# Pooled attention and an MLP mixer: u kept as pairs of token chunks, and its transpose by way of memory

## The chip, the cores and the metric

The kernel runs on one core of one Trainium2 chip. The metric is the device time of one execution in microseconds, the median of several runs. The engines are called PE (TensorE matmuls; PEld its weight loads), DVE (VectorE), ACT (ScalarE), POOL (GpSimd) and SP (SyncE, which here only issues DMAs).

## What is computed

Eight batches (B = 8), eight heads, 576 tokens, 64 features a head. Keys and values are pooled by 8 along the sequence, attention runs over the 72 pooled keys, and its output x (576 tokens x 512 features per batch) goes through a mixer: a token MLP, then a channel MLP, each with a residual.

```python
def _attn_ref(q, k, v):
    k_p = k.reshape(B, H, Sp, pool, D).mean(axis=3)
    v_p = v.reshape(B, H, Sp, pool, D).mean(axis=3)
    scores = scale * np.matmul(q, k_p.transpose(0, 1, 3, 2))
    ...
    return np.matmul(attn, v_p)

def _moe_ref(x, w_tok1, w_tok2, w_ch1, w_ch2):
    xt = x.transpose(0, 2, 1)
    h = np.maximum(xt @ w_tok1, 0.0) @ w_tok2
    u = x + h.transpose(0, 2, 1)
    h2 = np.maximum(u @ w_ch1, 0.0) @ w_ch2
    return u + h2
```

w_tok1 is 576 x 256, w_tok2 256 x 576, w_ch1 512 x 1536, w_ch2 1536 x 512. Inputs and output are float32; inside, operands are bf16 and sums float32.

## The kernel before

**Tiling.** The 576 tokens of a batch are 64 x 9: token p * 9 + r. A chunk c (0 to 3) holds the 128 tokens with r = 2c and 2c + 1; the 64 tokens with r = 8 are the batch's tail. Tails of two batches fill one 128-row tile ("xt", then a row of `u_tails`), so that after eight batches the tails make four chunks of a ninth unit of work.

**Stages of a batch.** Scores and exp (`s0` to `s3`), attention output (`av0` to `av4`, PE at L317, DVE at L329 and L335), token MLP (`at0`, `at1`: L363, L354), and u (`u0` to `u4`: two matmuls at L378 and an add on DVE at L379 for each chunk). For the tails, `u4` is done once for two batches, with four matmuls whose weights `w_tok2t` are zero in the other batch's 64 columns.

**uT.** The channel MLP needs u with features on the partitions. Batch 0 gets it another way; batches 1 to 3 by PE transposes (`t0` to `t4`, L388, weights = u, and a DVE copy, L389). Batches 4 to 7 go through memory: `M0`, `M2` and (odd batches) `M4` spill u and the pair of tails to the DRAM tile `mem` (L397); `M` reads it back in four DMAs (L404), each for a quarter of the features, in runs of 128 elements, to `v`; `T0` to `T4` are DVE 32x32 block transposes from `v` to `uT` (L411, on 32-bit pairs of features) and `uT_tails` (L417, on bf16). Because a 32-bit element holds two neighbouring features of one token, `uT` of these batches has two features side by side, and `moving` (L464 to L468) reads every second element.

**Units.** `unit(n)` is the channel MLP of batch n, for n = 8 that of the tails. First product: `l1_tile` (from L470), 48 matmuls of 128 x 512 at L473 into 12 tiles, each evicted with a relu by ACT to `GT` (L477). Second product: unit 0 does it plainly (L496); units 1 to 8 (`unit_fast`, from L536) use seven block products instead of eight, in a Strassen-like scheme: `product` issues 84 matmuls of 128 x 256 at L545, whose weights are 128-column slices of `GT` or of sums of its parts (`fast["S"]`, in the tile "area", made by DVE at L516 and L523 in `g_sums`), and `plus` (L566) adds u and partial results on DVE. `store` (L487) writes two DMAs per pair of chunks from SP; in unit 8 the last two chunks are stored by `store_part` (L578), each half of the columns and each chunk by itself.

**Order.** It is written out by hand: each engine executes in the order in which the program issues. A unit is a generator that yields some 48 times (after every two matmuls of the first product, every four of the second); at the yield with number i, the steps that a table lists for i are issued: steps of the next batch (no mark), of this one ("<"), of the one after next (">"), loads ("lk3": load k of batch n + 3), `g_sums` ("=1a") and `gate` ("g0"), which lets POOL go on. `FIRST`, `SECOND`, `THIRD` and `LAST` are the tables of units 0, 1, 2 and 8, `LATER` that of units 3 to 7. So unit n works on batch n and prepares u and uT of batch n + 1 and the attention of batch n + 2. `u4`, `t4`, `M4` and `T4` are left out for even batches. SP's queue holds the spills, the reads and the stores in program order; POOL's holds the loads of inputs and the pooling.

Of the kernel before, what the change touches and what calls it, by code (L numbers as in the profile page):

```python
# [22 lines left out]
FIRST = {0: "<u0", 2: "<u3", 6: "k1", 10: "lv2", 15: "K0 Q0", 16: "kpT Q1 lk3", 18: "V0 s1 <u2", 20: "s0",  # L23
         22: "lq3 v1 s2", 24: ">K0 s3", 25: "av1", 26: "av4", 27: "<u1 av3 av2", 30: ">K1", 32: "av0", 36: "at0 at1",
         38: "u3 >V0", 40: "u4 u0", 44: "lv3 u2 u1", 45: "t3 t0", 46: "t1", 47: "t2 t4"}
SECOND = {4: "g0", 7: ">K0 kpT", 8: "Q1", 9: "Q0", 11: "s2", 12: ">Q0", 13: ">Q1", 14: "v1 =3a s0", 15: "lv3 lk3",
          16: "s1", 17: "=1a", 18: "s3 =3b", 19: "av1", 20: "av3", 21: "av2", 22: "lq3", 23: ">K1 av0", 24: "av4",
          26: "g1", 27: "=1b", 28: ">kpT =2a", 29: "at0", 30: ">s3", 31: "=2b", 32: "=4b at1 =4a", 34: ">s2",
          36: "u2", 38: ">V0", 39: "u0 >s1 u3", 40: "t2", 41: "u1 t3", 42: ">s0 >V1 t0 t1"}
THIRD = {0: ">K0 av4 lk3 lq3", 2: "av3", 4: ">K1", 6: "av0", 9: "av2", 10: ">V0 av1", 12: "=3b", 14: "at0 at1",  # L30
         15: "=3a", 16: ">kpT", 17: "g0", 18: ">Q0", 19: "=1a u3 >s1", 20: ">Q1", 23: "u1 >s3 =2a", 24: "u0 =1b u2",
         25: "=2b t1", 26: ">s0", 28: "u4 >s2 =4b", 29: ">V1", 30: "=4a g1", 33: "t0", 34: "t2 >av3", 35: "t3",
         37: ">av4", 39: "t4 >av1", 41: "lv3", 42: ">av2", 44: ">av0"}
LATER = {0: ">Q0", 6: "=3a >K0", 7: "at0 at1", 8: ">K1 >kpT", 9: ">V0 u1 u0 >Q1", 10: "u3 >s1", 11: ">V1 u4",
         12: "u2", 13: ">s0", 14: "M0", 15: "M4 M2", 16: "M", 17: ">s3 lk3", 18: "=3b", 20: "=1a", 21: "g0",
         22: ">av3 =2a", 23: "=1b", 24: "lq3", 25: "=2b", 27: ">s2 =4a", 28: "=4b", 31: "g1 >av2", 36: ">av4",
         38: "T1 T3", 39: "T2", 40: "T0", 43: ">av0", 44: ">av1 lv3 T4"}
LAST = {14: "=3b", 22: "=1a", 24: "=2a =1b", 25: "=4a", 28: "=2b", 31: "=4b", 34: "=3a"}
PLANS = {0: FIRST, 1: SECOND, 2: THIRD, 8: LAST}


@with_exitstack
def kernel(
# [44 lines left out]
    w_tok2t = singles.tile([P, 2, 2, P], BF16)  # L88
# [8 lines left out]
    u_tails = singles.tile([P, 4, DM], BF16)  # L97
# [50 lines left out]
    def permute_tok2():  # L148
        src = f2.rearrange("t m (p r) -> t m r p", r=BR)
        dst = w_tok2.rearrange("t m (r p) -> t m r p", p=BP)  # L150
        for m in range(2):
            nc.gpsimd.tensor_copy(out=dst[:, m], in_=src[:, m])
        for half in range(2):
            nc.gpsimd.tensor_copy(out=w_tok2t[:, :, half, half * BP:(half + 1) * BP], in_=w_tok2[:, :, 8 * BP:S])
# [25 lines left out]
    def batch_steps(b):  # L180
# [19 lines left out]
        def late(key):  # L200
            if key not in st:
                pool, shape = {"x": (mix, [P, 4, DM]), "u": (mix, [P, 4, DM]), "uT": (mix, [P, 4, 4 * P]),
                               "AT": (att, [P, 2, DM]), "qD": (att, [P, 2, S, 2])}[key]
                st[key] = pool.tile(shape, BF16, name=key)
            return st[key]

        def parts(src):
            return src.rearrange("p (m k) -> p k m", k=4)

# [158 lines left out]
        def u(c):  # L368
            def go():
                ps = ps_one.tile([P, 512], FP32, name="p1")  # L370
                if c < 4:
                    mms = [(w_tok2[:, m, c * P:(c + 1) * P], st["AT"][:, m, :]) for m in range(2)]
                    dst, x = late("u")[:, c, :], st["x"][:, c, :]
                else:
                    mms = [(w_tok2t[:, m, half, :], tails[b // 2, half][:, m, :]) for half in range(2) for m in range(2)]
                    dst, x = u_tails[:, b // 2, :], st["xt"]
                for i, (w, a) in enumerate(mms):
                    nc.tensor.matmul(out=ps, lhsT=w, rhs=a, start=(i == 0), stop=(i == len(mms) - 1))  # L378
                nc.vector.tensor_tensor(out=dst, in0=ps, in1=x, op=ALU.add)  # L379
            return go  # L380

        def uT(c):
            def go():
                src = st["u"][:, c, :] if c < 4 else u_tails[:, b // 2, :]
                dst, o = (late("uT"), c * P) if c < 4 else (uT_tails, b // 2 * P)
                ps = ps_one.tile([P, 4, P], BF16, name="p1")
                for kk in range(4):
                    nc.tensor.transpose(out=ps[:, kk, :], in_=parts(src)[:, kk], identity=ident)  # L388
                nc.vector.tensor_copy(out=dst[:, :, o:o + P], in_=ps)  # L389
            return go  # L390

        def spill(i):
            def go():
                if "mem" not in st:
                    st["mem"] = hbm.tile([5, P, DM], BF16, name="mem")
                src = st["u"][:, 2 * i:2 * i + 2, :] if i < 2 else u_tails[:, b // 2:b // 2 + 1, :]
                nc.sync.dma_start(out=st["mem"][2 * i:min(2 * i + 2, 5)].rearrange("c p n -> p c n"), in_=src)  # L397
            return go

        def quads():  # L400
            n = 4 + par
            st["v"] = swap.tile([P, 4 * 5, P], BF16, name="v")
            for a in range(4):
                nc.sync.dma_start(out=st["v"][32 * a:32 * a + 32, 0:4 * n, :],  # L404
                                  in_=st["mem"][0:n, :, a * P:(a + 1) * P].rearrange("c (i t) f -> t (c i) f", i=4))

        def blocks(c):
            def go():
                if c < 4:
                    st["paired"] = True  # L410
                    nc.vector.transpose(  # L411
                        out=late("uT").rearrange("f k n -> f (k n)").bitcast(U32).rearrange(
                            "f (k c a t) -> f k c a t", k=2, c=4, a=4)[:, :, c].rearrange("f k a t -> f a k t"),
                        in_=st["v"][:, 4 * c:4 * c + 4, :].bitcast(U32).rearrange("t a (f k) -> t a k f", k=2))
                    return
                dst, o = uT_tails, b // 2 * P
                nc.vector.transpose(out=dst[:, :, o:o + P].rearrange("f k (a t) -> f a k t", a=4),  # L417
                                    in_=st["v"][:, 4 * c:4 * c + 4, :].rearrange("t a (f k) -> t a k f", k=4))
# [32 lines left out]
        for c in range(5):  # L451
            name[f"av{c}"], name[f"u{c}"], name[f"t{c}"] = av(c), u(c), uT(c)
            name[f"aw{c}"] = av(c, True)
            name[f"at_{c}"], name[f"T{c}"] = at_tile(c), blocks(c)
# [4 lines left out]
        name["M"] = quads  # L459
# [4 lines left out]
    def moving(u):  # L464
        if "paired" not in u:
            return [u["uT"][:, kk, :] for kk in range(4)]
        pairs = u["uT"].rearrange("f k n -> f (k n)").rearrange("f (k n e) -> f k n e", k=2, e=2)
        return [pairs[:, kk // 2, :, kk % 2] for kk in range(4)]  # L468
# [20 lines left out]
    def unit_plain(n, u):  # L489
        uT = moving(u)  # L490
        for m in range(NM):
            yield from l1_tile(n, m, uT)
        for c in range(4):
# [8 lines left out]
            nc.vector.tensor_tensor(out=o[:, c % 2], in0=ps, in1=u["u"][:, c, :], op=ALU.add)  # L502
# [33 lines left out]
    def unit_fast(n, u):  # L536
        last = n == B
        uT = moving(u)
# [3 lines left out]
        def product(ps, a, w, start, after, split=False):  # L542
            for i in range(2):
                for m in range(NH):
                    nc.tensor.matmul(out=ps[i] if split else ps[:, i], lhsT=a(m)[:, i * P:(i + 1) * P], rhs=w(m),  # L545
# [26 lines left out]
        def store_part(cols):  # L572
            def go(i):
                if not last:
                    return
                c = 2 + i
                for half in range(2):
                    (nc.scalar if half else nc.sync).dma_start(  # L578
                        out=out[2 * c + half].rearrange("(p r) n -> p r n", r=BR)[:, 8, cols],
                        in_=ob[half * BP:(half + 1) * BP, i, cols])  # L580
# [3 lines left out]
        u1, u2 = u["u"][:, 0:2], u["u"][:, 2:4]  # L584
# [18 lines left out]
        if last:  # L603
            yield from product(x, lambda m: SG[:, 2, m], lambda m: TW[:, 2, m], False,
                               plus(ob[:, :, hi], x, s5, store_part(hi)), True)
            yield from product(x, lambda m: GT[:, NH + m, hi], lambda m: TW[:, 3, m], False,
                               plus(ob[:, :, lo], x, u2[:, :, lo], store_part(lo)), True)
# [25 lines left out]
    def unit(n, at):  # L633
        if n + 2 < B:
            batches[n + 2][0]()
        st = batches[n][2] if n < B else dict(uT=uT_tails, u=u_tails)
# [5 lines left out]
        for i, _ in enumerate((unit_fast if n >= 1 else unit_plain)(n, st)):  # L642
            for s in at.get(i, "").split():
                if s[0] == "=":
                    g_sums(s[1:])
                    continue
                if s[0] == "l":
                    load(s[1], n + int(s[2]))
                    continue
                if s[0] == "g":  # L650
                    gate()
                    continue
                ahead = {"<": 0, ">": 2}.get(s[0], 1)
                s = s.lstrip("<>")
                if n + ahead < B and ((n + ahead) % 2 or s not in ("u4", "t4", "M4", "T4")):
                    batches[n + ahead][1][s]()

    with tc.manual_schedule(engines={PE, POOLE, DVE, ACT, SYNC}):
# [10 lines left out]
        nc.vector.memset(w_tok2t, 0.0)  # L669
# [13 lines left out]
        for n in range(B + 1):  # L683
            unit(n, PLANS.get(n, LATER))
# [30 lines left out]
```

## Time and profile before

| | |
|---|---|
| median of 3 runs | 278.35 us (278.29 to 280.8) |
| span of the profiled execution | 276.3 us |
| granted clock of TensorE | 0.995 of full speed |
| PE / DVE / ACT / POOL busy | 261.1 / 193.0 / 113.6 / 144.8 us |
| DMA | 36,455 packets, 32.71 MB, 13,776 of them under 512 bytes |

The costliest groups of the steps concerned (line, engine, operation, destination and sources, shapes, count; then busy us and mean ns of one; then idle time of the engine before them and what ended it):

```profile
L473 PE MATMUL p<-uT,w_ch 128*128 128x512 bf16 x366 | 91.8, 383 | 2.7 <-DVE uT L411 1.1
...
L545 PEld LDWEIGHTS <-area 128*128 128x128 bf16 x384 | 36.6, 98 | 5.1 <-issue 0.5
L545 PE MATMUL p<-area,area 128*128 128x256 bf16 x288 | 36.2, 273 | 0.0
...
L379 DVE TENSOR_TENSOR u<-p,x 128x512 bf16<-128x512 f32 x32 | 21.5, 684 | 13.5 <-PE p L378 13.3
...
mem<-u SPq DMA_DIRECT2D x8, 256.0 KB, 2.1
v<-mem SPq DMA_DIRECT2D x8, 160.0 KB, 6.7
v<-mem SPq DMA_DIRECT2D x8, 128.0 KB, 5.3
```

A matmul's duration in such a row includes its way through the array; matmuls overlap, and what one costs TensorE is the distance from one start to the next. In the last three rows the numbers are the KB of one DMA and the median time from issue to landing.

### The profile page before, as it was taken

What the parts mean: (1) busy time and instruction counts of PE and PEld (TensorE: products, weight loads), DVE (VectorE), ACT (ScalarE), POOL (GpSimd) and SP (SyncE); (2) the same over time, 40 slices, a digit from 0 to 9 for tenths busy, and PEclk for the clock granted to TensorE, in tenths of its full rate; (3) what the DMA queues carried; (4) which work ended last, traced back from release to release, by engine and by line L of the source; (5) the groups of instructions that cost most, each with busy time, mean ns of one, the idle gap of its engine ahead of it and who ended that gap; (6) DMA issues with size and microseconds to landing.
All of it is one profiled execution on the core that took longest, in us unless ns stands there. A gap on an engine that the chain in (4) does not pass through costs nothing.

```text
span 276.3 us, 5208 instructions
## 1 busy us (share of the span) xinstructions
PE 261.1 (95%) x2064; PEld 156.1 (57%) x2092; DVE 193.0 (70%) x378; ACT 113.6 (41%) x200; POOL 144.8 (52%) x138
## 2 busy tenths in 40 slices
PE   7889889989999999999998999999999999999991
PEld 2765334444466654784486437843784486485581
DVE  5465987389999879897487857775794667263281
ACT  2453671107723456305920574057406412603600
POOL 8594793975989986299629962996000000000000
PEclk9999999999999999999999999999999999999997
DMA  7999999937590690074497549952305253204006
GB/s 161 193 202 206 205 205 186 202 68 152 76 168 14 118 203 4 6 114 123 109 171 131 155 108 170 169 154 80 76 2 152 97 96 79 77 0 132 23 0 152
DMA packets 36455, 32.71 MB, mean 118 GB/s; under 512 B 13776, under 2 KB 30032, under 8 KB 36432
## 3 DMA queue, kind: packets, MB, share of 16 engines
q0 software_dynamic: 18672, 17.64, 41.7%
q1 hardware_dynamic: 17440, 14.49, 20.7%
q8 instruction: 16, 0.26, 0.4%
q10 hardware_dynamic: 320, 0.26, 0.3%
q14 instruction: 7, 0.06, 0.1%
HBM read 38.21 MB, written 11.80 MB: 181 GB/s over the span
## 4 chain that ended last, share of the span: by engine, by line
PE 58%; DMA 17%; DVE 14%; POOL 4%; issue 2%; ACT 2%; SPq 2%; DVEq 0%; POOLq 0%; ACTq 0%
PE p L473 23%; PE p L545 18%; DMA v<-mem 8%; PE p L378 5%; DMA kr<-in_k_dram 5%; PE p L363 5%; DVE area L516 4%; DMA area<-in_moe_w_tok_dram 3%; PE p L496 3%; PE p L317 2%; PE p L279 2%; DMA mem<-u 2%; SPq L404 2%; DVE u L379 1%; DVE x L335 1%
## 5 line engine op out<-in xcount | busy, mean ns | idle before, releaser
L477 ACT ACTIVATE GT<-p 128x512 bf16<-128x512 f32 x108 | 64.4, 596 | 97.9 <-PE p L473 58.1
L473 PE MATMUL p<-uT,w_ch 128*128 128x512 bf16 x366 | 91.8, 383 | 2.7 <-DVE uT L411 1.1
L473 PEld LDWEIGHTS <-w_ch 128*128 128x128 bf16 x432 | 39.4, 97 | 48.8 <-issue 5.8
L631 POOL COPY flag<-flag 1x1 f32<-1x1 f32 x14 | 3.5, 247 | 81.7 <-DVE flag L630 81.7
L285 ACT ACTIVATE ex<-p 72x576 bf16<-72x576 f32 x56 | 33.1, 642 | 18.0 <-PE p L279 17.9
L545 PEld LDWEIGHTS <-area 128*128 128x128 bf16 x384 | 36.6, 98 | 5.1 <-issue 0.5
L545 PE MATMUL p<-area,area 128*128 128x256 bf16 x288 | 36.2, 273 | 0.0
L171 POOL TENSOR_TENSOR t<-t 72x512 f32<-72x512 f32 x25 | 34.3, 1372 | 2.0
L379 DVE TENSOR_TENSOR u<-p,x 128x512 bf16<-128x512 f32 x32 | 21.5, 684 | 13.5 <-PE p L378 13.3
L545 PEld LDWEIGHTS <-GT 128*128 128x128 bf16 x288 | 27.1, 98 | 6.2 <-issue 1.4
L170 POOL TENSOR_TENSOR t<-kr 72x1024 f32<-72x1024 bf16 x13 | 27.7, 2130 | 4.8 <-DMA kr<-in_k_dram 4.3
L170 POOL TENSOR_TENSOR t<-vr 72x1024 f32<-72x1024 bf16 x12 | 25.7, 2143 | 0.7
L545 PE MATMUL p<-w_ch,GT 128*128 128x256 bf16 x192 | 23.8, 273 | 0.1
L566 DVE TENSOR_TENSOR o<-p,s 128x512 f32<-128x512 f32 (+1 forms) x32 | 20.6, 663 | 2.6 <-PE p L545 2.6
L523 DVE TENSOR_TENSOR area<-GT 128x768 bf16<-128x768 bf16 x16 | 10.3, 642 | 16.8 <-ACT GT L477 16.7
L335 DVE TENSOR_TENSOR x<-p,den 128x512 bf16<-128x512 f32 x30 | 20.7, 691 | 1.0
L566 DVE TENSOR_TENSOR s<-p,u 128x512 f32<-128x512 f32 x28 | 19.2, 685 | 3.2 <-PE p L545 3.1
L516 DVE TENSOR_TENSOR area<-GT 128x768 bf16<-128x768 bf16 x16 | 13.5, 849 | 9.6 <-ACT GT L477 9.6
L317 PEld LDWEIGHTS <-ex 72*128 72x128 bf16 x320 | 14.9, 98 | 7.1 <-DVE x L335 1.3
L378 PE MATMUL p<-AT,w_tok 128*128 128x512 bf16 x63 | 17.8, 379 | 0.4 <-DVE u L379 0.4
L317 PE MATMUL p<-vp,ex 72*128 72x65 bf16 x320 | 16.8, 194 | 1.1 <-DVE x L335 0.3
L354 ACT ACTIVATE AT<-p 128x512 bf16<-128x512 f32 x15 | 9.0, 597 | 20.8 <-PE p L363 18.1
(102 smaller groups left out, 322.9 us busy)
## 6 DMA issues: line engine op xcount, KB each, us to landing
out_dram<-o SPq DMA_DIRECT2D x34, 256.0 KB, 3.5
kr<-in_k_dram POOLq DMA_DIRECT2D x7, 576.0 KB, 11.0
qb<-in_q_dram POOLq DMA_DIRECT2D x7, 576.0 KB, 12.4
vr<-in_v_dram POOLq DMA_DIRECT2D x7, 576.0 KB, 8.7
w_ch<-in_moe_w_ch_dram POOLq DMA_DIRECT2D x6, 512.0 KB, 13.5
mem<-u SPq DMA_DIRECT2D x8, 256.0 KB, 2.1
v<-mem SPq DMA_DIRECT2D x8, 160.0 KB, 6.7
v<-mem SPq DMA_DIRECT2D x8, 128.0 KB, 5.3
```

The source lines that it names most:

```text
L170: eng.tensor_tensor(out=t4[:, 0:n], in0=t[:, hs, 0:4], in1=t[:, hs, 4:8], op=ALU.add)
L171: eng.tensor_tensor(out=t4[:, 0:n, 0:2], in0=t4[:, 0:n, 0:2], in1=t4[:, 0:n, 2:4], op=ALU.add)
L285: nc.scalar.activation(out=exv[:, h:h + 2], in_=pss[a][0:SP, :, 0:SH], func=AF.Exp, scale=scale)
L317: nc.tensor.matmul(out=halves[h // 4][:, (h % 4) * (D + 1):(h % 4 + 1) * (D + 1)], lhsT=st["ex"][:, h * S + n0:h * S + n0 + P], rhs=st["vp ...
L335: nc.vector.tensor_tensor(out=dst.rearrange("p (a h d) -> p a h d", a=2, d=D), in0=view[:, :, :, 0:D], in1=den[rows, :, :, None].broadcast ...
L378: nc.tensor.matmul(out=ps, lhsT=w, rhs=a, start=(i == 0), stop=(i == len(mms) - 1))
L379: nc.vector.tensor_tensor(out=dst, in0=ps, in1=x, op=ALU.add)
L473: nc.tensor.matmul(out=ps, lhsT=w_ch1[:, kk, m * P:(m + 1) * P], rhs=uT[kk], start=(kk == 0), stop=(kk == 3))
L477: nc.scalar.activation(out=GT[:, m, :], in_=ps, func=AF.Relu)
L516: nc.vector.tensor_tensor(out=out, in0=a, in1=b, op=ALU.subtract)
L545: nc.tensor.matmul(out=ps[i] if split else ps[:, i], lhsT=a(m)[:, i * P:(i + 1) * P], rhs=w(m), start=start and m == 0 and (i == 0 or spli ...
L566: nc.vector.tensor_tensor(out=out[:, i], in0=ps[i] if type(ps) is list else ps[:, i], in1=other[:, i], op=ALU.add)
```

## The change

u of two chunks is kept interleaved: element (p, i, f, e) is feature f of chunk 2i + e, so that a 32-bit element holds one feature of two tokens. The spill writes each pair as one run of 2 KB a partition; the reads take runs of 256 elements (512 bytes); the 32-bit block transposes then give a `uT` in which each feature is a contiguous row, and the columns alternate between the two chunks. `moving` goes; in units 4 to 8 the weights of the second product are read with `chunk`, every second column. Everything else that reads u reads it in 4-byte steps (`rows_of`, `rows`); the PE transposes of batches 1 to 3 read it in 16-byte steps where they read it in 8-byte steps before.

All tails go through memory now, four batches at a time: `M4`, `MT`, `T4` and `T5` for batch 3 (in units 2 and 3, for batches 0 to 3) and for batch 7 (in units 6 and 7). `t4` goes. `u4` uses the plain `w_tok2` with two column tiles of 64, and `w_tok2t` goes. In unit 8 the last stores cover both chunks: three DMAs of ACT and one of SP instead of four and four. The tables are written out per unit with the batch's number ("4.M0"); apart from the tails' steps the order on each engine stays.

```diff
-    w_tok2t = singles.tile([P, 2, 2, P], BF16)
...
-    u_tails = singles.tile([P, 4, DM], BF16)
+    u_tails = singles.tile([P, 2, DM, 2], BF16)
...
-        for half in range(2):
-            nc.gpsimd.tensor_copy(out=w_tok2t[:, :, half, half * BP:(half + 1) * BP], in_=w_tok2[:, :, 8 * BP:S])
...
+        def rows_of(c):
+            if c == 4:
+                return u_tails[:, b // 4, :, b // 2 % 2]
+            return late("u")[:, c // 2, :, c % 2]
...
                 else:
-                    mms = [(w_tok2t[:, m, half, :], tails[b // 2, half][:, m, :]) for half in range(2) for m in range(2)]
-                    dst, x = u_tails[:, b // 2, :], st["xt"]
+                    mms = []
+                    for m in range(2):
+                        for half in range(2):
+                            nc.tensor.matmul(out=ps[half * BP:(half + 1) * BP], lhsT=w_tok2[:, m, 8 * BP:S],
+                                             rhs=tails[b // 2, half][:, m, :], start=(m == 0), stop=(m == 1),
+                                             tile_position=(0, half * BP), skip_group_check=True)
+                    x = st["xt"]
...
-                nc.vector.tensor_tensor(out=dst, in0=ps, in1=x, op=ALU.add)
+                nc.vector.tensor_tensor(out=rows_of(c), in0=ps, in1=x, op=ALU.add)
...
         def spill(i):
             def go():
                 if "mem" not in st:
-                    st["mem"] = hbm.tile([5, P, DM], BF16, name="mem")
-                src = st["u"][:, 2 * i:2 * i + 2, :] if i < 2 else u_tails[:, b // 2:b // 2 + 1, :]
-                nc.sync.dma_start(out=st["mem"][2 * i:min(2 * i + 2, 5)].rearrange("c p n -> p c n"), in_=src)
+                    st["mem"] = hbm.tile([3, P, 2 * DM], BF16, name="mem")
+                src = st["u"][:, i] if i < 2 else u_tails[:, b // 4]
+                nc.sync.dma_start(out=st["mem"][i], in_=src.rearrange("p f e -> p (f e)"))
...
-            for a in range(4):
-                nc.sync.dma_start(out=st["v"][32 * a:32 * a + 32, 0:4 * n, :],
-                                  in_=st["mem"][0:n, :, a * P:(a + 1) * P].rearrange("c (i t) f -> t (c i) f", i=4))
+                for a in range(4):
+                    src = st["mem"][i0:i1, :, a * 2 * P:(a + 1) * 2 * P].rearrange("c (i t) f -> t (c i) f", i=4)
+                    dst = st["v"][32 * a:32 * a + 32, i0:i1].rearrange("t c i f -> t (c i) f")
+                    nc.sync.dma_start(out=dst, in_=src)
...
+                nc.vector.transpose(
+                    out=dst.rearrange("f k n -> f (k n)").bitcast(U32).rearrange(
+                        "f (k o a t) -> f o a k t", k=4, o=4, a=2)[:, o],
+                    in_=st["v"][:, i, 2 * h:2 * h + 2, :].bitcast(U32).rearrange("t a (f k) -> t a k f", k=4))
...
-    def moving(u):
...
+    def chunk(u, c, a):
+        return a[:, c::2] if "paired" in u else a[:, c * P:(c + 1) * P]
+
+    def rows(u, i):
+        return u["u"][:, i].rearrange("p f e -> p e f")
...
-                    nc.tensor.matmul(out=ps[i] if split else ps[:, i], lhsT=a(m)[:, i * P:(i + 1) * P], rhs=w(m),
+                    nc.tensor.matmul(out=ps[i] if split else ps[:, i], lhsT=chunk(u, i, a(m)), rhs=w(m),
...
-        def store_part(cols):
+        def store_part(cols, engines):
             def go(i):
-                if not last:
+                if i == 0:
                     return
-                c = 2 + i
                 for half in range(2):
-                    (nc.scalar if half else nc.sync).dma_start(
-                        out=out[2 * c + half].rearrange("(p r) n -> p r n", r=BR)[:, 8, cols],
-                        in_=ob[half * BP:(half + 1) * BP, i, cols])
+                    engines[half].dma_start(
+                        out=out.rearrange("(c h) (p r) n -> h p c r n", h=2, r=BR)[half][:, 2:4, 8, cols],
+                        in_=ob[half * BP:(half + 1) * BP, :, cols])
...
-                               plus(ob[:, :, hi], x, s5, store_part(hi)), True)
+                               plus(ob[:, :, hi], x, s5, store_part(hi, (nc.scalar, nc.scalar))), True)
...
-                               plus(ob[:, :, lo], x, u2[:, :, lo], store_part(lo)), True)
+                               plus(ob[:, :, lo], x, u2[:, :, lo], store_part(lo, (nc.sync, nc.scalar))), True)
```

In the tables: unit 2 has `3.M4` at 30 and `3.MT` at 35 (before, `t4` of batch 3 stood at 39), unit 3 has `3.T4` at 2 and `3.T5` at 3, unit 6 has `7.M4` at 17 and `7.MT` at 20, unit 7 has `7.T4` at 8 and `7.T5` at 12; `M4` and `T4` of batch 5 are gone (before, `M4` stood at 15 between `M0` and `M2`, and `T4` at 44).

## The prediction

> **What bounds the kernel now.** I read the page's head, busy times and chain of waits first, to see which engine sets the end; then the chain in order of time; then who waits; then TensorE's instructions in order of time, for the price of single steps.
>
> ```profile
> span 276.3 us, 5208 instructions
> ...
> PE 261.1 (95%) x2064; PEld 156.1 (57%) x2092; DVE 193.0 (70%) x378; ACT 113.6 (41%) x200; POOL 144.8 (52%) x138
> ...
> PE 58%; DMA 17%; DVE 14%; POOL 4%; issue 2%; ACT 2%; SPq 2%; DVEq 0%; POOLq 0%; ACTq 0%
> ```
>
> TensorE is busy for 95% and carries 58% of the chain, so time comes off mostly where TensorE time or a TensorE wait goes. The chain in order of time shows the places that the change touches:
>
> ```profile
> 60.63 0.33 DVE uT_tails L389
> ...
> 133.61 2.15 DMA mem<-u
> ...
> 137.74 10.92 DMA v<-mem
> 148.78 1.43 DVE uT L411 x4
> ...
> 231.34 10.51 PE p L473 x46
> ...
> 251.29 10.09 PE p L473 x46
> ...
> 270.61 0.42 DVE o L566
> ```
>
> From 57 to 88 us the chain runs through VectorE, afterwards through TensorE. The two L473 lines are the first product of unit 7 (moving operand in 4-byte steps, the "paired" uT) and of unit 8 (uT_tails, contiguous), with the same 46 records: 10.51 against 10.09 us. At 133 to 150 us the chain leaves TensorE for the bounce through memory. How much TensorE loses by that is in the list of waits:
>
> ```profile
> DVE uT L411 <- DMA v<-mem: 2.9, 2, 1.5
> ...
> PE p L473 <- DVE uT L411: 1.1, 2, 0.7
> ```
>
> Only two of the four bounces are late (units 4 and 5), and TensorE loses 1.1 us. Last, TensorE's own instructions (start, length, line, shape, count):
>
> ```profile
> 42.32 0.43 PE L317 MATMUL p<-vp,ex 72*128 72x65 bf16 x8
> ...
> 57.87 0.61 PE L388 MATMUL p<-ident,u 128*128 128x128 bf16 x8
> ...
> 86.99 0.59 PE L378 MATMUL p<-AT,w_tok 128*128 128x512 bf16 x2 [0.39 <-DVE u L379]
> 87.51 0.45 PE L279 MATMUL p<-qD,kD 32*72 32x288 bf16 x8
> 87.89 0.61 PE L378 MATMUL p<-AT,w_tok 128*128 128x512 bf16 x2
> ...
> 263.84 2.78 PE L545 MATMUL p<-area,area 128*128 128x256 bf16 x24
> ```
>
> A group's length is its starts plus one full duration. Eight L317 with contiguous 128-column weights: (0.43 - 0.19) / 7 = 33 ns from start to start. Eight L388, whose weights are read in 8-byte steps: (0.61 - 0.22) / 7 = 56 ns, no more than the contiguous transposes of L260 (five in 0.45 us: 58 ns). L545: (2.78 - 0.27) / 23 = 109 ns.
>
> **The change, part by part.**
>
> *First product, units 4 to 7.* The moving operand becomes contiguous. (10.51 - 10.09) / 46 = 9.1 ns a matmul, 48 matmuls in each of four units: 192 x 9.1 = **-1.75 us**, all on TensorE. ScalarE evicts one tile in 0.60 us against 0.86 us of matmuls, so it doesn't become the bound.
>
> *Second product, units 4 to 8.* The weights GT and area are now read in 4-byte steps: 84 loads x 5 units = 420. A contiguous load lasts 98 ns, one in 8-byte steps (L388) 112 to 116 ns, and both start 56 ns apart without delay. Here a load has 109 ns of matmul to hide behind. **0**; bounds 0 to 15 ns each, 6.3 us (a rival below). No gain: hidden loads give none.
>
> *u written in pairs.* 32 adds write bf16 in 4-byte steps. The trace has no such write. Nearest rows: the same add, contiguous (L379), 684 ns; the same size with float output, which steps 4 bytes an element (L566 o<-p,s), 679 ns. I take **0**. Upper bound: twice the pace per element; 512 against 256 elements are 0.68 against 0.42 us, so 0.53 us more an add, of which some six lie in VectorE's stretch: +3.2 us. The adds of L566 that read u in steps have the float operand as their row: 685 against 679 ns, 0.
>
> *Transposes of u for batches 1 to 3.* They stay on TensorE, but their weights go from 8- to 16-byte steps. 98 to 114 ns came with 8-byte steps, four times the distance; twice that distance again gives, as an estimate from these rows, some 130 ns. Added to the 33 ns at which contiguous loads follow each other that is about 65 against 56 ns: 48 x 9 = 0.43 us if exposed, half of it beside VectorE's stretch: **+0.2**, bounds 0 to 2.7 (56 ns more each; see the rivals).
>
> *The bounce.* Each of its four reads has 256 packets of 512 bytes instead of 512 of 256. In unit 3 the reads ran from 135.83 to 148.66 us, while the DMA engines were fully busy (share 0.96 to 1.35 in the windows from 136 to 148). VectorE stood 1.5 us before the transposes, so 12% off 12.8 us is enough; half the packets give up to 6.4. Bounds 0 to -1.1; I take **-1.1**, near the end at which the packets count. Next late is nothing: TensorE's last L317 end as unit 4 starts.
>
> *Tails, b = 1 and 3.* Their four transposes and one VectorE copy each go: 0.33 us on VectorE's chain at 60.63, and 4 x 56 = 0.22 us of TensorE at 119.4: **-0.55**. In their place batch 3 issues one spill and four reads on SP in unit 2. SP waits for the u_tails add (done at 113.8), then for the spill's landing (1.7 us in the row of mem<-u_tails), and issues for some 2 us until 118; the stores of unit 2 queue behind and are due at 122: covered by 4 us. T4 and T5 (0.40 us each, from L411) stand before the first difference of GT on VectorE in unit 3, at 125.6; VectorE idles 0.44 and 1.06 us there, which covers 0.8. Were the reads to land after 125.6, the GT sums, the copy of kD and batch 4's adds would queue behind; reads of 64 KB begun at 116 have 9 us, where 128 KB took up to 10.9 in the fuller stretch. For batch 7 the reads sit on SP behind its quads (about 222) and ahead of stores due at 231; T4, T5 replace one 0.70 us transpose where VectorE idles 1.5 to 2.1 us. **0**.
>
> *u4 in two column tiles.* Before: 4 matmuls, 0.86 us. No column tile is in the trace; the nearest row is the four row tiles of L279. They run side by side (8 matmuls of 288 columns as 2 x 0.12 us), but the switch costs: L378 x2 from 86.99 fill to 87.42, L279 starts at 87.51 (0.09), is through at 87.75 and L378 starts at 87.89 (0.14, part of it first loads). Two columns side by side: 2 x 0.216 + 0.23 = 0.66, -0.2 each; one after the other: +0.23 each. Four of them, all on the chain: **-0.75**, bounds -0.8 to +0.9; I take side by side, as the row tiles are. The Trainium skill ("TensorEngine Tiling (Array Packing)", Key Properties) says that changing the tiling mode drains the array and that tiles run independently; the 0.09 and 0.14 us agree with the first, and if only the drain held, this term would be +0.9.
>
> *The end.* Before, eight part-stores queue on SP and ACT:
>
> ```profile
> L578 SPq DMA_DIRECT2D out_dram<-o x4: 588/725/1390, 270.0 to 273.2; - x4
> ...
> DMA to landing us min/median/max: 2.1/3.2/3.7
> ```
>
> The last add ends at 271.03, yet the last issue starts at 273.2 and lands after 2.1, near 275.3. Now the last two issue at 271.1, one on each queue, the upper columns' two being issued by ACT from 269.7 to 270.9. Landing by 3.3 to 3.7 us: 274.4 to 274.8. **-0.65**, bounds -0.9 to 0.
>
> *Start.* Two copies (0.53 us) leave GpSimd at 18.3 and a 0.27 us memset leaves VectorE; GpSimd then stands waiting at 25 and 29 us (1.6 and 3.5 us) anyhow: 0. If the loads behind came sooner by 0.53 nothing waits on them.
>
> Sum: -1.75 - 1.1 - 0.55 - 0.75 - 0.65 + 0.2 = -4.6 us on the span of 276.3, that is 271.7. The median of the runs, 278.35, is 2.05 above that span; I keep this distance: **273.7 us**.
>
> **The rivals.**
>
> *Slower: stepped weight loads that no longer hide.* Place: the 420 loads of L545. If a load holds its port for all its length, 98 ns fit under 109 and 112 to 116 don't; at the bound of 15 ns each, 6.3 us, the time is 278.35 - 4.6 + 6.3 = 280.0; from 11 ns on it is slower than before, from 18 on by over 1%. For it: the stepped moving operand did pay. Against: L388 starts such loads every 56 ns. 12%, 8 of it beyond 1%.
>
> *Column tiles one after the other.* +0.9 instead of -0.75: 275.4. For it: different data would have to enter the same rows. Against: the row tiles. 12%.
>
> *16-byte transposes at half pace.* If each costs a full 56 ns more, 48 x 56 = 2.7 us instead of 0.2; some lies under VectorE: 275.5 to 276.3. Against: the small step from 98 to 112 ns. 9%. The Trainium skill ("SBUF — State Buffer", the note on cachelines) holds that a 16-byte line needs two hits to hide its latency; 8-byte steps have two, 16-byte steps one, and no run shows such a step yet.
>
> *Tail reads late in unit 3.* If they take the 10.9 us of the worst read, from 117.5 on, VectorE stands until 128.4, 2.8 us, of which 1.5 is idle anyway: +1.3, 275.0. Against: the share there is about 0.6. 7%.
>
> If the change doesn't make the bounce shorter, 1.1 is missing: 274.8, inside the forecast's own range.
>
> **How the numbers follow.** The forecast has 60%, its own range 272 to 275. Two kernels within 1% count as the same here: 275.57 to 281.13. Faster: 60, 8 of the column tiles (some lands above the line), 1 of the transposes, 7 of the tail reads: 76%. Same: 4 + 8 + 4 = 16%. Slower: 8%. The range, 271.6 to 277.0, takes in the u adds' bound (273.7 + 3.2 = 276.9) and all rivals but the first, and below the forecast every term at its better end plus some luck in how transfers meet.
>
> **What would show it.** Right: L473 starts 216 ns apart in all units; L545 stays at 109 ns; no wait of L473 for the transposes of v; u4 takes about 0.66 us; the last landing stands some 3.5 us behind the last add. Wrong: L545 above 115 ns, u adds above 0.75 us, L388 above 65 ns from start to start, VectorE waiting for v early in unit 3.

## The result and the profile after

| | before | this |
|---|---|---|
| median | 279.06 us (19 executions, 277.15 to 281.03) | 281.71 us (19 executions, 279.88 to 284.18) |
| span of the profiled execution | 276.3 us | 279.9 us |
| granted clock of TensorE in it | 0.995 | 0.992 |
| ratio | | 1.009, 95% interval 1.0062 to 1.0118 |

The change makes the kernel slower by 0.9%, by 3.6 us in the two spans, where 4.6 us less was forecast. A ratio, here and below, leaves out executions over 1.5% longer than the kernel's fastest, so it isn't always the quotient of the medians. The head of the page after (busy us, share of the span, instructions; then the shares of the chain):

```profile
span 279.9 us, 5195 instructions
...
PE 260.9 (93%) x2057; PEld 156.5 (56%) x2084; DVE 201.0 (72%) x377; ACT 113.5 (41%) x200; POOL 145.0 (52%) x136
...
PE 58%; DMA 17%; DVE 12%; POOL 4%; ACT 3%; issue 3%; SPq 1%; DVEq 0%; POOLq 0%; ACTq 0%
```

TensorE works as long as before (260.9 against 261.1 us), so the added time is waiting. VectorE has one instruction less and is busy 8.0 us longer. A sum over the whole kernel doesn't say where; a table by unit does. It is made from TensorE's timeline: from the first matmul of one unit's first product to that of the next, in us. "e1" and "e4" are two experiments below.

| unit | before | this | difference | e1 | e4 |
|---|---|---|---|---|---|
| start of unit 0 | 25.11 | 25.51 | +0.40 | | |
| 0 | 35.57 | 35.60 | +0.03 | 34.60 | 34.38 |
| 1 | 31.66 | 36.88 | **+5.22** | 32.19 | 31.78 |
| 2 | 30.45 | 30.03 | -0.42 | 29.83 | 29.80 |
| 3 | 27.46 | 27.56 | +0.10 | 27.58 | 26.97 |
| 4 | 28.66 | 28.00 | -0.66 | 27.81 | 27.45 |
| 5 | 27.25 | 26.84 | -0.41 | 26.85 | 26.80 |
| 6 | 24.72 | 24.52 | -0.20 | 24.51 | 24.07 |
| 7 | 19.97 | 19.54 | -0.43 | 19.54 | 19.53 |
| 8, to the start of its last matmul | 19.44 | 19.44 | 0 | 19.44 | 19.44 |
| from there to the end | 5.97 | 5.99 | +0.02 | | |

The differences add up to the 3.6 us. All the loss is in unit 1; units 2 to 7 gain 2.0 us. (Unit 0 varies by up to 1.6 us among kernels that are the same there, so nothing is read from it.) The chain of waits in order of time (start, length, what) has two entries at 72 us that the chain before doesn't have, and the entries that answer to those shown of before:

```profile
72.08 3.38 DVE area L530
75.45 1.53 DVE area L523
...
142.44 10.84 DMA v<-mem
153.31 2.22 DVE uT L420 x4
...
235.38 10.09 PE p L480 x46
...
254.91 10.09 PE p L480 x46
```

The first products of units 7 and 8 now take the same 10.09 us: this part of the forecast came as worked out. The bounce's last read is as long as before (10.84 against 10.92 us), and the four block transposes after it take 2.22 us where they took 1.43. The list of waits (us in total, times, longest):

```profile
PE p L313 <- DVE x L331: 4.0, 2, 3.6
...
PE p L480 <- DVE uT L420: 1.5, 3, 0.8
DVE uT L420 <- DMA v<-mem: 1.3, 2, 0.8
```

The first line is new. TensorE stands 3.6 us at once before an attention output (L313), because VectorE normalises the one before (L331) late. VectorE does that right after three sums of GT (`=3a`, `=1a`, `=3b`: L523, L530, L523). Those three are where unit 1 loses its time. VectorE's timeline before (start, length, line, operation), `=1a` and `=3b`:

```profile
71.85 0.55 DVE L523 TENSOR_TENSOR area<-GT 128x768 bf16<-128x768 bf16 x1
72.32 0.55 DVE L516 TENSOR_TENSOR area<-GT 128x768 bf16<-128x768 bf16 x1
```

and after, all three:

```profile
71.47 0.55 DVE L523 TENSOR_TENSOR area<-GT 128x768 bf16<-128x768 bf16 x1
72.08 3.38 DVE L530 TENSOR_TENSOR area<-GT 128x768 bf16<-128x768 bf16 x1
75.38 1.61 DVE L523 TENSOR_TENSOR area<-GT 128x768 bf16<-128x768 bf16 x1
```

The same instruction takes 3.38 instead of 0.55 us and the next 1.61 instead of 0.55: 3.9 us on VectorE's chain. Beside it, after, the tile of GT that `=1a` reads, on ScalarE, and GpSimd's work:

```profile
71.45 0.59 ACT L484 ACTIVATE GT<-p 128x512 bf16<-128x512 f32 x1
```

```profile
72.14 0.74 POOL L121 DMA_DIRECT2D qb<-in_q_dram  x1
72.87 2.15 POOL L161 TENSOR_TENSOR t<-kr 72x1024 f32<-72x1024 bf16 x1
```

Before, the same tile and the same pooling:

```profile
71.03 0.59 ACT L477 ACTIVATE GT<-p 128x512 bf16<-128x512 f32 x1
```

```profile
72.78 2.15 POOL L170 TENSOR_TENSOR t<-kr 72x1024 f32<-72x1024 bf16 x1
```

Sums that follow one another start 0.47 us apart, so `=1a` would have started at 71.94. The GT tile ends at 72.04, and `=1a` starts at 72.08, 0.14 us late. Before, that tile ended at 71.62 and VectorE came at 71.85: no wait. GpSimd's pooling began at 72.78, when `=1a` was done (72.40) and `=3b` had been under way since 72.32, and both kept their 0.55 us. After, `=1a` is recorded from 72.08, 0.79 us before the pooling, and yet ends at 75.46, 0.44 us behind the pooling's 75.02. The reading to test: VectorE comes a little too early, has to wait, and GpSimd gets ahead of it.

### The profile page after: what moved, and what is told of

It reads as the page before. It is cut to its first block, busy times and chain, and to the rows that moved or that the text cites. A ratio compares the mean times of both kernels' runs of the same rounds, so it can differ in the third digit from the quotient of the medians.

```text
span 279.9 us, 5195 instructions
## 1 busy us (share of the span) xinstructions
PE 260.9 (93%) x2057; PEld 156.5 (56%) x2084; DVE 201.0 (72%) x377; ACT 113.5 (41%) x200; POOL 145.0 (52%) x136
## 4 chain that ended last, share of the span: by engine, by line
PE 58%; DMA 17%; DVE 12%; POOL 4%; ACT 3%; issue 3%; SPq 1%; DVEq 0%; POOLq 0%; ACTq 0%
PE p L480 24%; PE p L552 16%; DMA v<-mem 7%; DMA kr<-in_k_dram 5%; PE p L359 5%; PE p L379 4%; DMA area<-in_moe_w_tok_dram 3%; PE p L503 3%; DVE area L523 3%; PE p L313 2%; DVE uT L420 2%; DVE u L380 2%; ACT ex L281 2%; PE p L275 2%; DMA mem<-u 1%
## 5 line engine op out<-in xcount | busy, mean ns | idle before, releaser
L480 PE MATMUL p<-uT,w_ch 128*128 128x512 bf16 x366 | 91.0, 383 | 3.1 <-DVE uT L420 1.5
L480 PEld LDWEIGHTS <-w_ch 128*128 128x128 bf16 x432 | 39.6, 98 | 48.7 <-issue 7.4
L380 DVE TENSOR_TENSOR u<-p,x 128x512 bf16<-128x512 f32 x32 | 22.7, 729 | 13.2 <-PE p L379 13.0
L530 DVE TENSOR_TENSOR area<-GT 128x768 bf16<-128x768 bf16 x16 | 13.1, 818 | 16.3 <-ACT GT L484 16.1
L313 PE MATMUL p<-vp,ex 72*128 72x65 bf16 x320 | 17.3, 197 | 4.7 <-DVE x L331 4.0
L313 PEld LDWEIGHTS <-ex 72*128 72x128 bf16 x320 | 15.4, 100 | 11.1 <-DVE x L331 5.2
L331 DVE TENSOR_TENSOR x<-p,den 128x512 bf16<-128x512 f32 x30 | 20.8, 692 | 1.0
L523 DVE TENSOR_TENSOR area<-GT 128x768 bf16<-128x768 bf16 x16 | 14.5, 914 | 7.4 <-ACT GT L484 7.3
L379 PE MATMUL p<-AT,w_tok 128*128 128x512 bf16 x63 | 17.9, 380 | 0.4 <-DVE u L380 0.4
```

The costliest lines, as they stand in the source:

```text
L313: nc.tensor.matmul(out=halves[h // 4][:, (h % 4) * (D + 1):(h % 4 + 1) * (D + 1)], lhsT=st["ex"][:, h * S + n0:h * S + n0 + P], rhs=st["vp ...
L331: nc.vector.tensor_tensor(out=dst.rearrange("p (a h d) -> p a h d", a=2, d=D), in0=view[:, :, :, 0:D], in1=den[rows, :, :, None].broadcast ...
L380: nc.vector.tensor_tensor(out=rows_of(c), in0=ps, in1=x, op=ALU.add)
L480: nc.tensor.matmul(out=ps, lhsT=w_ch1[:, kk, m * P:(m + 1) * P], rhs=uT[kk], start=(kk == 0), stop=(kk == 3))
L523: nc.vector.tensor_tensor(out=out, in0=a, in1=b, op=ALU.subtract)
```

## The experiments

The texts set down ahead of the runs name their theories by letters. A is the reading just given; A1 says that VectorE comes too early because t4's copy is gone from its queue, A2 that another part of the change shifts it. C is that the bounce is long because of the loads beside it. Each run's ratio is to the kernel before on the same chip.

### Holding GpSimd back until the sums are done

```diff
-    {4: "g", ... 18: "2.s3 =3b", 19: "2.av1", ...
+    {4: "g", ... 18: "2.s3 =3b g", 19: "2.av1", ...
```

Unit 1's table gets one more gate, which lets GpSimd go on behind `=3b`; all else is the changed kernel.

> The changed kernel with one more gate in unit 1, behind the GT difference '=3b': GpSimd's second pooling of k waits until VectorE's three GT sums are done. Theory A (in unit 1 VectorE's GT sums meet GpSimd's pooling: '=1a' 3.38 instead of 0.55 us, '=3b' 1.61 instead of 0.55): these two take about 0.55 us again, unit 1 falls from 36.9 to about 31.7 us, and the kernel comes to 276 to 277.5 us, 0.98 to 0.995 of the kernel before. Theory B (unit 1 is long for the change's own work: adds that write u in steps, transposes in 16-byte steps): unit 1 stays at 36 to 37 us, the ratio stays at 1.005 to 1.012.

Measured: 275.86 us (4 executions) against 279.71 (13), ratio 0.9893 (0.981 to 0.9977); span 273.8 us. Unit 1 is back at 32.19 us. VectorE's timeline of it:

```profile
70.50 0.55 DVE L523 TENSOR_TENSOR area<-GT 128x768 bf16<-128x768 bf16 x1
71.09 0.56 DVE L530 TENSOR_TENSOR area<-GT 128x768 bf16<-128x768 bf16 x1
71.57 0.55 DVE L523 TENSOR_TENSOR area<-GT 128x768 bf16<-128x768 bf16 x1
```

`=1a` starts 0.59 us behind `=3a` instead of 0.47: it waits here too, 0.12 us, and takes 0.56 us. The wait by itself costs next to nothing; the loss needs GpSimd's work as well. The gate isn't free: GpSimd comes later, so that `=1b`, further on, meets the end of its pooling and takes 0.96 us instead of 0.55.

### The same gate in the kernel before

```diff
-          16: "s1", 17: "=1a", 18: "s3 =3b", 19: "av1", ...
+          16: "s1", 17: "=1a", 18: "s3 =3b g0", 19: "av1", ...
```

> The kernel before with the same gate. Theory A: in the profile of before the three sums did not meet the pooling, so the gate changes little where that holds; unit 1 stays at 31 to 32 us and the ratio is 0.99 to 1.00 (below 1 only so far as some runs of the kernel before meet too). Theory B: 1.00.

Measured: 281.39 us (10 executions) against 279.71 (13), ratio 1.0036 (0.9988 to 1.0084), unit 1 32.20 us; `=1b` takes 1.08 us instead of 0.54 here too. The gate is no gain of its own; in the changed kernel it is worth something only because it undoes a loss.

### TensorE later by two matmuls, in the kernel before

```diff
+        for _ in range(2 if (n, m) == (1, 0) else 0):
+            nc.tensor.matmul(out=ps, lhsT=w_ch1[:, 0, 0:P], rhs=uT[0], start=True, stop=True)
```

This makes the tiles of GT in unit 1 later by some 0.4 us and leaves VectorE's order alone.

> The kernel before with two matmuls of 512 columns more at the head of unit 1's first product (their result is overwritten): TensorE, and with it ScalarE's GT tiles, come 0.43 us later against GpSimd. Theory A: '=1a' waits for its GT tile, GpSimd starts its pooling first, unit 1 grows by 3 to 5.5 us, ratio 1.010 to 1.020. Theory B: unit 1 grows by 0 to 0.5 us, ratio 1.000 to 1.002.

Measured: four timed executions of 284.5 to 287.9 us, ratio 1.0222 (1.0117 to 1.0327), a little more than was expected. A fifth, the profiled one, took 1515 us and tells nothing; e3b is the same kernel, profiled again.

> The kernel before with two matmuls more at the head of unit 1's first product, for its profile. Theory A: one of the three GT sums of unit 1 stands for 2.5 to 3.5 us beside GpSimd's pooling, unit 1 takes 35 to 37 us instead of 31.7. Theory B: unit 1 32 us, and the added time is elsewhere.

Measured: 286.03 us, span 284.1, unit 1 37.80 us. `=1a` stands idle 0.17 us for GT (last bracket), starts 0.72 us behind `=3a` instead of 0.47, and then takes six times as long:

```profile
72.22 3.27 DVE L525 TENSOR_TENSOR area<-GT 128x768 bf16<-128x768 bf16 x1 [0.17 <-ACT GT L479]
```

So the loss appears in the kernel before with none of the change in it. Two matmuls of 0.43 us together cost unit 1 6.1 us.

### A filler in place of t4's copy, in the changed kernel

```diff
-    ... 46: "1.t1", 47: "1.t2"},
+    ... 46: "1.t1", 47: "1.t2 pad"},
...
+                elif s == "pad":
+                    nc.vector.memset(uT_tails[:, 0:2, 0:384], 0.0)
```

> The changed kernel with a memset of 0.4 us on VectorE where the copy of the removed t4 stood, at the end of unit 0 (it zeroes part of uT_tails, which is written again later). Theory A1 (taking that copy away moved VectorE, and GpSimd behind it, about 0.35 us ahead of TensorE and ScalarE, so that '=1a' finds its GT tile unfinished and GpSimd's pooling goes first): with the memset the GT sums of unit 1 take 0.55 us each again, unit 1 falls from 36.9 to about 32, ratio 0.985 to 0.997. Rival A2 (the meeting comes from the steps that became slower, the u adds of 0.73 us and the 16-byte transposes, not from the copy): the memset only adds 0.4 us, ratio 1.008 to 1.014.

Measured: 276.38 us (10 executions) against 278.70 (19), ratio 0.9885 (0.9849 to 0.992), span 273.7, unit 1 31.92 us. The filler takes 0.38 us of VectorE and saves 5 us of unit 1. `=1a` now comes without a wait, 0.47 us behind `=3a` and 0.31 us behind the end of its GT tile (71.70). It is done 0.39 us before the same pooling begins (72.95 to 75.09):

```profile
72.01 0.55 DVE L530 TENSOR_TENSOR area<-GT 128x768 bf16<-128x768 bf16 x1
```

Three of its ten executions, not in the ratio, took 279.2 to 280.5 us. Whether the sums were caught again in those was not seen, since one execution has a profile.

### That one step alone, in the kernel before

```diff
-         ... 45: "t3 t0", 46: "t1", 47: "t2 t4"}
+         ... 45: "t3 t0", 46: "t1", 47: "t2"}
...
-          ... 41: "u1 t3", 42: ">s0 >V1 t0 t1"}
+          ... 41: "u1 t3", 42: ">s0 >V1 t0 t1", 43: "<t4"}
```

t4 of batch 1 goes from the end of unit 0 to the end of unit 1, and nothing else of the change is made.

> The kernel before with t4 of batches 0 and 1 (four transposes and the 0.41 us copy on VectorE) moved from the end of unit 0 to the end of unit 1; nothing else of the change. Theory A1 (the place of that copy decides whether '=1a' of unit 1 comes ahead of GpSimd's pooling): '=1a' stands some 3 us, unit 1 takes 35.5 to 38 us instead of 31.7 and the ratio is 1.010 to 1.022. Rival A2 (it needs the steps that the change made slower): unit 1 takes 31.5 to 32 us, ratio 0.999 to 1.002.

Measured: 285.01 us (4 executions) against 280.85 (6), ratio 1.017 (1.0063 to 1.0277), unit 1 38.07 us.

```profile
72.12 3.35 DVE L523 TENSOR_TENSOR area<-GT 128x768 bf16<-128x768 bf16 x1
75.39 1.61 DVE L516 TENSOR_TENSOR area<-GT 128x768 bf16<-128x768 bf16 x1
```

Taking t4 from that place is enough to bring on the whole loss; A1 holds and A2 falls. The run moves t4's four matmuls as well as its copy; that the copy alone counts is shown by the filler, which only VectorE runs.

### Block transposes that read contiguously

```diff
-                    in_=st["v"][:, i, 2 * h:2 * h + 2, :].bitcast(U32).rearrange("t a (f k) -> t a k f", k=4))
+                    in_=st["v"][:, i, 2 * h:2 * h + 2, :].bitcast(U32).rearrange("t a (k f) -> t a k f", k=4))
```

The features reach uT in another order than w_ch1 expects, so the channel MLP multiplies them by other weights' rows; the work is the same in kind and amount.

> The changed kernel with VectorE's block transposes T0 to T5 reading v contiguously instead of in 16-byte steps (the features of uT of batches 4 to 7 and of the tails then stand in another order than the rows of w_ch1; all the work is done). If the 16-byte step is what made them 0.61 instead of 0.40 us, they take 0.40 again, the four ahead of a unit 1.43 instead of 2.22 us, units 3 to 6 lose up to 0.8 us each where TensorE waits for them, 1 to 2.4 us in all: ratio about 1.001 to 1.005. If the length comes from the way the results are written (64-byte runs over the columns), they stay at 0.6 us and the ratio stays at 1.009.

Measured: 273.21, 282.09, 279.55 and 279.56 us; no ratio. Its profile is that of the first (span 271.4 us), and there `=1a` came at 70.71, behind the GT tile's 70.56, and took 0.55 us: this kernel has neither gate nor filler, and in this execution it escaped. Up to unit 3 it does the same as the changed kernel, so the loss of unit 1 doesn't come in every execution; what made VectorE 0.25 us later here isn't known, and the other three have no profile. The line of the block transposes (duration min/median/max in ns), after:

```profile
L420 DVE STREAM_TRANSPOSE uT<-v x16: 589/602/652, 153.3 to 234.3; 128x256 uint32<-128x256 uint32 x16
```

and in this kernel:

```profile
L420 DVE STREAM_TRANSPOSE uT<-v x16: 401/403/445, 146.7 to 225.7; 128x256 uint32<-128x256 uint32 x16
```

The step of 16 bytes in the read costs 0.2 us an instruction. TensorE no longer waits for them (1.1 us in the gate kernel, nothing here), and units 3 to 6 take 0.61, 0.36, 0.05 and 0.44 us less than in the gate kernel: 1.46 us. Against the filler's kernel, whose unit 4 took 27.46 us, it is 1.10 us.

### The bounce without loads beside it

```diff
-                    if s[0] == "l":
+                    if s[0] == "l" and int(b) >= 6 and s[1] in "kq":
+                        loaded[int(b), s[1]] = loaded[int(b) - 2, s[1]]
+                    elif s[0] == "l":
```

On top of the gate, q and k of batches 6 and 7 aren't loaded; those of 4 and 5 are used again.

> The changed kernel with the gate, without the loads of q and k of batches 6 and 7 (those of batches 4 and 5 are used in their place, so these batches' output differs). Theory C (the bounce shares the DMA engines with those loads by bytes, so that halving its packets could not shorten it): in unit 3, without them, the last of the four reads lands 3 to 5 us after its issue instead of 10.8, and VectorE no longer waits for v. Rival D (the reads of v are slow by themselves, 32 partitions and one run after another): it still takes over 8 us.

Measured: 276.19 us in one execution, span 274.2. The reads of the bounce in unit 3, from issue to landing, after:

```profile
L408 SPq DMA_DIRECT2D v<-mem x4: 319/512/587, 141.0 to 142.4; - x4
...
DMA to landing us min/median/max: 7.7/11.0/11.2
```

and without the loads:

```profile
L408 SPq DMA_DIRECT2D v<-mem x4: 319/447/450, 136.8 to 138.1; - x4
...
DMA to landing us min/median/max: 2.4/2.8/3.0
```

Before they took 7.3 to 10.9 us. The bounce's length is the loads' doing, and VectorE no longer waits for v: D falls. That the share goes by bytes, the other half of C, isn't shown by this run. Unit 3 gains 0.7 us on the gate kernel (26.86 us); unit 4's 27.46 us is what two kernels with the loads have too (the filler's and the next one).

### The last stores on both queues

```diff
-                               plus(ob[:, :, hi], x, s5, store_part(hi, (nc.scalar, nc.scalar))), True)
+                               plus(ob[:, :, hi], x, s5, store_part(hi, (nc.scalar, nc.sync))), True)
```

On top of the gate, the upper columns' two stores go out on one queue each.

> The changed kernel with the gate, and the last store of the upper columns split over ACT and SP instead of both halves on ACT. If ACT's queue set the end (three stores in a row, the last issued 0.8 us after the last add), the last landing comes 3.2 to 3.5 us after the last add instead of 3.9 and the time is 0.3 to 0.6 us below that of the kernel with the gate alone. If the landing sets it, nothing changes. Ratio to the kernel before 0.985 to 0.993 either way.

Measured: 276.21 us (10 executions) against 278.70 (19), ratio 0.9902 (0.9876 to 0.9929); span 273.6 us against 273.8 with the gate alone. The last landing follows the last add by 3.65 instead of 3.85 us, which is between the two forecasts, and the end of the span by 4.94 instead of 5.20. The queue was some 0.2 us of the end and the landing is the rest.

### GpSimd held back longer

```diff
-    ... 24: "2.av4", 26: "g", 27: "=1b", ... 32: "=4b 2.at1 =4a", ...
+    ... 24: "2.av4", 27: "=1b", ... 32: "=4b 2.at1 =4a g", ...
```

On top of the previous kernel, unit 1's next gate goes behind the remaining sums, which also met GpSimd's work (2.39 and 1.02 us, and 2.94 us for two of them).

> The changed kernel with the gate behind '=3b' and the split last store, and with unit 1's second gate moved from slot 26 to behind '=4a' in slot 32, so that GpSimd's pooling of v starts after the last GT sums of unit 1, some 4 us later. If what VectorE loses beside the pooling there (2.39 + 1.02 + 2.94 us for four sums that take 0.55 alone) is on the path, unit 1 falls by 2 to 4 us and the ratio is 0.975 to 0.985. If the later pooling of v, or of k behind it, is waited for in unit 2, unit 2 grows by as much and the ratio stays at 0.987 to 0.993.

Measured: 275.35 us (4 executions) against 280.85 (6), ratio 0.9845 (0.9723 to 0.9966). These four sums take 0.55 us each, and unit 1 0.74 us less, but units 2 and 3 take 0.49 and 0.43 us more: in the new place VectorE waits for TensorE, and GpSimd's later start is paid for afterwards. The spans are 273.5 and 273.6 us; nothing is gained that the trace shows.

## Why the prediction was wrong

**The step that failed.** "*Tails, b = 1 and 3.* Their four transposes and one VectorE copy each go: 0.33 us on VectorE's chain at 60.63 ...: **-0.55**". The instructions did go. But the step priced a removed 0.33 us by itself, and never asked what comes earlier by it on VectorE and on GpSimd, which VectorE's gate lets go. Both moved forward against ScalarE: counted from unit 1's first matmul, `=3a` starts at 10.70 us before and at 10.37 after, 0.33 us earlier, while the GT tile ends at 10.94 both times. So `=1a` met an unwritten tile and then GpSimd's work. Instead of -0.33 us at that place there was +5.2 us in unit 1. The moved t4 alone does it (unit 1 38.07 us), the filler undoes it (31.92), and so does the gate (32.19). No rival held this, though the profile before had what it takes: a margin of 0.23 us between the GT tile's end (71.62) and the sum that reads it (71.85), less than the 0.33 us to be taken away ahead of it.

Put in order by this margin (from the GT tile's end to 0.47 us behind the start of `=3a`, negative where VectorE has to wait), the runs agree. With 0.31 us (filler), 0.23 (before) and 0.15 (the contiguous transposes) `=1a` takes 0.55 us. With -0.10 (after), -0.12 (t4 moved) and -0.21 (two matmuls) it takes 3.38, 3.35 and 3.27 us. With -0.10 and GpSimd held back it takes 0.56.

What a sum pays beside the pooling can be read in the whole of both traces, and a wait isn't needed for it. This sum of the kernel before, `=2a`, waits for nothing and begins 0.13 us after a pooling on GpSimd:

```profile
78.20 2.11 POOL L170 TENSOR_TENSOR t<-vr 72x1024 f32<-72x1024 bf16 x1
```

```profile
78.33 2.39 DVE L516 TENSOR_TENSOR area<-area,GT 128x768 bf16<-128x768 bf16 x1
```

It ends 0.41 us behind that pooling. In the two traces 28 sums of GT begin while a `tensor_tensor` of GpSimd runs, most of them without a wait, and every one ends 0.41 to 0.55 us behind it; all others but one take 0.54 to 0.56 us. The Trainium skill ("SBUF — State Buffer", Who interferes with whom) has the ground for it: VectorE and GpSimd share a port pair, locked for a whole instruction, over which a `tensor_tensor` with both inputs in SBUF contends with a GpSimd instruction that reads SBUF, and the one issued first blocks the other. The 28 sums agree. So does a sum of unit 5 in the kernel with contiguous transposes, which got the pair itself: recorded 0.03 us behind a pooling's start (179.33), it took 0.56 us, and the pooling 2.58 instead of 2.11. The one other is `=1a` after. Its end 0.44 us behind the pooling's end agrees too. That it is recorded from 72.08, while the pooling is recorded from 72.87 only, agrees less: a sum that held the pair from 72.08 would have been done. What of GpSimd's work gets ahead in those 0.8 us no run tells. Nor is it shown that the waiting itself does it: in all three long cases `=1a` also starts within 0.06 us of the moment at which GpSimd begins to issue the load of q (72.14 after), and no run parts the two.

**Right.** *First product:* L480 at 10.09 us in unit 7 as in unit 8; units 5 and 7 gain 0.41 and 0.43 us, forecast 0.44 each (unit 6 only 0.20: its block transposes, below). *Second product:* loads in 4-byte steps last 98 ns as before, and 84 matmuls take 9.17 us; the first rival (12%) falls. *u4 in two column tiles:* the timeline of TensorE after, with the four u4 matmuls in the second line:

```profile
53.25 1.03 PE L503 MATMUL p<-w_ch,GT 128*128 128x512 bf16 x4
54.20 0.62 PE L374 MATMUL p<-AT,w_tok 128*64 128x512 bf16 x4
54.76 0.61 PE L379 MATMUL p<-AT,w_tok 128*128 128x512 bf16 x2
...
58.22 0.65 PE L387 MATMUL p<-ident,u 128*128 128x128 bf16 x8
```

The four of L503 before them hold TensorE until 53.25 + 4 x 0.216 = 54.11, and L379 starts at 54.76. The four u4 matmuls with the change of mode thus cost 0.65 us, 0.66 was forecast; one after the other they would cost 0.86 without it. The second rival falls. *Tail reads:* VectorE doesn't wait for them in unit 3, as forecast.

**Transposes of u at 16-byte steps.** The loads take 146 ns, 130 were estimated; the eight L387 above start (0.65 - 0.23) / 7 = 60 ns apart, 65 were forecast against 56 before. The third rival falls.

**Block transposes of v.** Not in the sum at all: T4 and T5 were priced "0.40 us each, from L411", although the change makes every one of these read in steps of 16 bytes. At 0.61 us, the four of a unit are 0.8 us longer, at the end of the bounce where TensorE waits for them. The Trainium skill ("SBUF — State Buffer", Specifications (TRN2), the row on cachelines), which the prediction brought in for TensorE's transposes alone, says that full pace needs at least two hits on each line of 16 bytes. The durations agree: 0.61 us where each line is read once, 0.40 in steps of 8 bytes, two hits to a line.

**The bounce: -1.1 forecast, nothing left of it at TensorE.** Its last read is as long as before, with half the packets (10.84 against 10.92 us). "Half the packets give" was the wrong idea. In two microseconds of unit 3 in which the reads run beside loads in packets of 1,024 bytes, the trace's records have 111 and 169 packets of 256 bytes before and 62 and 97 of 512 bytes after, each time beside 142 to 152 packets of loads: about as many bytes. That the reads get a share of the DMA engines by bytes is read from these counts; no run tests it. Without loads the reads land in 3 us. Still, v came earlier: the last read was issued sooner (14.4 instead of 15.0 us after the first matmul of unit 3, 15.5 instead of 17.0 in unit 4) and landed 0.6 and 1.6 us sooner, and VectorE's wait for v fell from 2.9 to 1.3 us in all. TensorE's wait for the transposes was 1.1 us and is 1.1 us in the gate kernel, because the transposes became longer by as much; with contiguous ones, and the same 1.3 us of waiting for v, TensorE waits for none.

**u in pairs.** The 32 adds take 729 ns instead of 684 (forecast: none more, bound 1,200); six in VectorE's stretch are 0.3 us.

**The end: -0.65 forecast, nothing measured in the span.** The landing stands 3.9 us behind the last add (4.2 before), but from the last add to the end of the span it is 5.25 against 5.23 us. The forecast took the landing for the end. Behind the last landing SP goes through the rest of its waits one by one, 0.06 us apart, ten of them where before there were five, and that swallows the 0.3 us.

Without the meeting, then, the change is worth -2.5 us in the span (273.8 with the gate; 273.7 with the filler) where -4.6 was forecast: 1.1% by the ratios, 0.8% by the medians of the filler's series (276.38 against 278.70). Units 1 to 8 gain 1.9 us with the gate and 2.5 us with the filler; the 1.1 to 1.5 us that contiguous block transposes would add are the largest part of what is missing from the forecast there. With the gate or the filler the changed kernel is faster than the one before.

## What to carry to other kernels

Where engines run in an order written by hand, an instruction removed from one of them moves every meeting behind it, and its price isn't its duration: look for the next instruction that becomes ready with a margin smaller than what is removed, and ask what another engine does at that moment. Look above all for sums on VectorE with both inputs in SBUF that begin while GpSimd pools, or that have to wait for an input while GpSimd has pooling lined up: here each of them stood until 0.4 us behind the pooling. A gate that holds GpSimd back until the sum is done took 2.8 us off `=1a` and put 0.4 us on a later sum. When a layout is changed for TensorE's sake, price each reader and writer of it at its new step, the transposes and the adds too.

## What the runs showed that was not expected

- A VectorE sum that came 0.14 us late, with a load and a pooling next on GpSimd, was 3.38 instead of 0.55 us long and the next 1.61: twenty times the delay on the first alone.
- A sum of GT that begins while GpSimd runs a `tensor_tensor` ends 0.41 to 0.55 us behind it (28 sums in the traces of before and after); the kernel before pays this too, 2.39 us for `=2a` of unit 1.
- The kernel before stands 0.23 us from this: two matmuls more (0.43 us) cost 2.2%.
- A block transpose of 128 x 256 32-bit elements takes 0.40 us where it reads contiguously or in steps of 8 bytes and 0.61 us in steps of 16. Weight loads take 98 ns contiguous and in 4-byte steps, 113 in 8-byte and 146 in 16-byte steps, and in the transposes they start 56 to 60 ns apart all the same.
- Doubling the runs of a transfer from 256 to 512 bytes left its landing where it was (10.9 and 10.8 us for the last read of unit 3) beside loads; without these it lands in 3.
